# One padded tile, one result tile and one transposing transfer for queries and keys in a clustered-attention kernel

## The chip, the cores and the metric

The kernel runs on one core of a Trainium2 chip. The metric is the time of one launch in microseconds of device time, as a median of runs. One execution was taken with the hardware profiler; its rows are quoted below. TensorE multiplies, VectorE, ScalarE and GpSimd do the elementwise work, and the sync engine (SP) issues almost all transfers, in order, on one queue.

## The reference

Sixteen heads (2 batches of 8), 768 positions, 64 columns. Each query and each key belongs to the centroid (of 16) with which it has the largest product. A query sees the keys of its own cluster only. Two dense layers with softplus, and two with a leaky rectifier, follow.

```python
q_assign = argmax(einsum('bhsd,hcd->bhsc', q_n, c_n)); k_assign = argmax(einsum('bhsd,hcd->bhsc', k_n, c_n))
mask = q_assign[:, :, :, None] == k_assign[:, :, None, :]
scores = where(mask, matmul(q, k.T) / sqrt(D), -1e9)
attn = exp(scores - max(scores)); attn = attn / (sum(attn) + 1e-9)
x = (attn @ v).transpose(0, 2, 1, 3).reshape(1536, 512)
x = softplus(x @ w_in) @ w_out            # 512 -> 2048 -> 512
out = leaky(x @ w_in2) @ w_out2           # 512 -> 2048 -> 512
```

The weights come in 64-bit floats, which the kernel decodes itself.

## The kernel before

Every fp32 operand is carried as two fp16 parts, a high one and the rest. A head goes through these steps (h is the head, 0 to 15; C = 6 blocks of 128 positions):

- `load(h)` brings queries and keys into `qk`.
- `split(h)`: ScalarE casts queries into the first 64 columns of a padded tile `nq` and keys into those of `nk` (line 294), GpSimd takes the rests (line 295), ScalarE copies the high parts (line 296); all four go into `n1`. One transposing transfer of twelve 128 x 128 blocks turns `n1` into `t1` (line 298; the profile calls it t<-n).
- `assign_mm(h)` and `assign_el(h)`: products with the centroids (line 307), the largest of 16 on VectorE, and the cluster as 16 columns of 0 or BIG, which ScalarE writes beside the high parts in `nq` and `nk` (lines 329 and 330). Two transposing transfers of six blocks each, `nq` to `tq` (line 333) and `nk` to `tk` (line 334). A query and a key of one cluster then get BIG more in their product than others.
- `emit_s1(h, c)`: the masked products of the high parts (line 346), of which VectorE takes row maxima (line 353). `emit_m(h)` writes these maxima into further rows of `tq` (lines 360 to 375), so that the next product subtracts them.
- `emit_s2(h, j)`: scores by two products (lines 393 and 394), their exponentials on ScalarE (line 400), the rests on GpSimd (line 402).
- `emit_pv`: products with the values (lines 416 to 434); `emit_empty(h)`: a last product that reads `tq` (line 452) and corrects rows whose cluster has no key.
- `emit_norm(h)`: division, and the result of two heads side by side in `xnh` and `xnl`. `emit_out` transposes each (line 456) into `xt_h[b]` and `xt_l[b]`, what the first dense layer reads (`layer_in`, line 698). `layer_mid` (line 711) is the second layer.

The order of each engine's instructions is fixed when the kernel is built: a planner simulates the program and takes, of what it believes ready, what has the lowest number in `at_pri`. Head h has numbers around h: its split at h - 2.5, its row maxima at h - 4, its scores at h. From head 8 on, steps of the dense layers of the first batch are mixed in (`moe_steps`). `w_step` loads and decodes one 512 KB piece of the first two layers' weights; two pieces can be in flight.

On the sync queue some transfers are ordered behind another one: `behind_tk(h)` puts what is issued under it behind the transfer kept in `tki[h]`, which is line 334's. Under it stand, in turn h, the loads of the values of head h + 2, the finished output pair, and the weight pieces of the turn; all pieces that are left in turn 11 stand behind `tki[13]`.

Tiles rotate. `BUFS` names for each tag how many tiles there are that last and how many only in heads 0 to 7 (`atile`): the turn goes round both kinds until head 7, then round the lasting ones. `tq` has (3, 2), `tk` (3, 1). The padded tiles are fixed ones (`padded`): `nq` (2, 2), `nk` (2, 1). A tile is taken over when its last reader is done; for `tq` that is line 452 of the head before in the turn, for `nq` and `nk` the transposing transfer.

Of the kernel before, what the change touches and what calls it, by code (L numbers as in the profile page):

```python
# [9 lines left out]
F16 = mybir.dt.float16  # L10
BF16 = mybir.dt.bfloat16
I32 = mybir.dt.int32
AF = mybir.ActivationFunctionType
ALU = mybir.AluOpType
# [4 lines left out]
BIG = 32768.0  # L19
# [3 lines left out]


BUFS = {
# [4 lines left out]
}  # L30
NQ_BUFS, NK_BUFS, V_BUFS = (2, 2), (2, 1), 3
PSUM_BUFS = {"as": 1, "s1": 2, "s2": 2}


# [1 line left out]
HI = ("AA", "AA", "AA", "AA", "AA", "AA")  # L36
DUP = ("AA", "AA", "AA", "AA", "AA", "AA")
# [14 lines left out]
def by_group(table, h):  # L52
    return table[min(h // 2, 4 + (h >= 12))]
# [3 lines left out]
def attn_moe_kernel(  # L57
# [12 lines left out]
    nc = tc.nc  # L70
    V, S, G, PE = nc.vector, nc.scalar, nc.gpsimd, nc.tensor
    B, H, SEQ, D = q.shape
    NCL = cen.shape[1]
    DM, DFF = w_in1.shape
    C = SEQ // 128
    KDM, KFF = DM // 128, DFF // 128
    NH = B * H
    TB = 384
    scale = 1.0 / float(D) ** 0.5
# [4 lines left out]
    const = ctx.enter_context(tc.tile_pool(name="const", bufs=1))  # L84
# [5 lines left out]
    ep = actx.enter_context(tc.tile_pool(name="ep", bufs=1, reuse_waits="tile"))  # L90
    acon = bctx.enter_context(tc.tile_pool(name="acon", bufs=1, side="right", reuse_waits="tile"))
# [6 lines left out]
    def atile(shape, dt, tag, h):  # L98
        late, early = BUFS[tag]
        n = turn[tag] = turn.get(tag, -1) + 1  # L100
        if h < H and early and n % (late + early) >= late:
            return ep.tile(shape, dt, tag=tag, name=tag, bufs=early)
        return at.tile(shape, dt, tag=tag, name=tag, bufs=late)
# [2 lines left out]
    w_inl = const.tile([128, KDM, DFF], F16, name="w_inl")  # L106
    w_outh = const.tile([128, KFF, DM], F16, name="w_outh")
    w_outl = const.tile([128, KFF, DM], F16, name="w_outl")
    xt_h = [const.tile([128, KDM, SEQ], F16, name=f"xth{b}") for b in range(B)]
    xt_l = [const.tile([128, KDM, SEQ], F16, name=f"xtl{b}") for b in range(B)]  # L110
    def padded(bufs, name):
        n, late = sum(bufs), bufs[0]
        tiles = [(acon if i < late else ep).tile([128, C, 128], F16, name=f"{name}_{i}") for i in range(n)]
        return tiles, [tiles[h % n if h < H else (h - H) % late] for h in range(NH)]

    nqs, nq_of = padded(NQ_BUFS, "nq")
    nks, nk_of = padded(NK_BUFS, "nk")
    v2s = [acon.tile([128, C, 2 * D + 1], F16, name=f"v2_{i}") for i in range(V_BUFS)]
    v32s = [acon.tile([128, C, D + 1], F32, name=f"v32_{i}") for i in range(V_BUFS)]
    mms = [acon.tile([128, C, 3], F32, name=f"mm{i}") for i in range(2)]  # L120
# [14 lines left out]
    mark, tki = {}, {}  # L135
    ld_t, tp1, tp2, tpq, p_t, xn_t, as_t, x_t, v_t, svs = ({} for _ in range(10))
# [141 lines left out]
    def load_v(h):  # L278
        b, hh = divmod(h, H)
        vv = v32s[h % V_BUFS][:, :, 0:D]  # L280
        nc.sync.dma_start(out=vv, in_=v[b, hh].rearrange("(p c) d -> p c d", c=C))
        v_t[h] = vv
# [5 lines left out]

    def split(h):
        qk = ld_t.pop(h)  # L290
        nq, nk = nq_of[h], nk_of[h]
        n1 = atile([128, C, 4, D], F16, "n1", h)
        for t_, n_ in enumerate((nq, nk)):
            (S.copy if by_group(HI, h)[t_] == "A" else V.tensor_copy)(out=n_[:, :, 0:D], in_=qk[:, t_])
            G.tensor_tensor(out=n1[:, :, 1 + t_, :], in0=qk[:, t_], in1=n_[:, :, 0:D], op=ALU.subtract)
            (S.copy if by_group(DUP, h)[t_] == "A" else V.tensor_copy)(out=n1[:, :, 3 * t_, :], in_=n_[:, :, 0:D])
        t = atile([128, 2 * C, 128], F16, "t1", h)
        nc.sync.dma_start_transpose(out=t, in_=n1.rearrange("p c s d -> p (c s d)"))
        tp1[h] = t
# [13 lines left out]
                )  # L313

    def assign_el(h):
        nq, nk = nq_of[h], nk_of[h]
        aps = as_t.pop(h)
        a, e = (aps[:, n:n + 2 * C * NCL].rearrange("p (i j) -> p i j", j=NCL) for n in (0, 2 * C * NCL))
        mx = atile([128, 2 * C, 1], F32, "mx", h)
        V.reduce_max(out=mx, in_=a, axis=AX)  # L320
        V.tensor_tensor(out=e, in0=a, in1=mx.to_broadcast([128, 2 * C, NCL]), op=ALU.is_equal)
        V.tensor_tensor(out=e, in0=e, in1=tab, op=ALU.mult)
        m2 = atile([128, 2 * C, 1], F32, "m2", h)
        V.reduce_max(out=m2, in_=e, axis=AX)
        oh = atile([128, C, 2, NCL], F16, "oh", h)
        V.tensor_tensor(
            out=oh.rearrange("p c t j -> p (c t) j"), in0=e, in1=m2.to_broadcast([128, 2 * C, NCL]), op=ALU.is_equal
        )
        S.activation(out=nq[:, :, D:D + NCL], in_=oh[:, :, 0, :], func=AF.Copy, scale=BIG, bias=-BIG)
        S.activation(out=nk[:, :, D:D + NCL], in_=oh[:, :, 1, :], func=AF.Copy, scale=BIG)  # L330
        tk = atile([128, C, 128], F16, "tk", h)
        t = atile([128, C, 128], F16, "tq", h)
        nc.sync.dma_start_transpose(out=t, in_=nq.rearrange("p c d -> p (c d)"))
        tki[h] = nc.sync.dma_start_transpose(out=tk, in_=nk.rearrange("p c d -> p (c d)"))
        tp2[h] = t, tk

    KS1 = D + NCL
    MR = 96
# [112 lines left out]
        for c in range(C):  # L451
            PE.matmul(out=xps[:, c * XW:(c + 1) * XW], lhsT=t[MR:KS2, c, :], rhs=r[MR:KS2, :], start=False, stop=(c == C - 1))

    def emit_out(b, hh, xh, xl):
        for src, dst in ((xh, xt_h[b]), (xl, xt_l[b])):
            nc.sync.dma_start_transpose(
                out=dst[:, hh // 2, :].rearrange("p (c r) -> p c r", c=C), in_=src.rearrange("p c d -> p (c d)")
            )

    outs_t = {}  # L460

    def emit_norm(h):
        b, hh = divmod(h, H)
        if hh % 2 == 0:
            xn_t[h // 2] = [atile([128, C, 128], F16, f"xn{n}", h) for n in "hl"]
        xh, xl = xn_t[h // 2]
        xps = x_t.pop(h)
        xv = xps[:, 0:C * XW].rearrange("p (c d) -> p c d", d=XW)
        dp = xps[:, C * XW:C * XW + C].unsqueeze(2)
        dd = atile([128, C, 1], F32, "dd", h)  # L470
        V.tensor_scalar(out=dp, in0=xv[:, :, D:XW], scalar1=1e-9, scalar2=1.0 / XS, op0=ALU.add, op1=ALU.mult)
        V.reciprocal(out=dd, in_=dp)
        y = atile([128, C, D], F32, "y", h)
        V.tensor_tensor(out=y, in0=xv[:, :, 0:D], in1=dd.to_broadcast([128, C, D]), op=ALU.mult)  # L474
        cs = slice((hh % 2) * D, (hh % 2) * D + D)
        S.copy(out=xh[:, :, cs], in_=y)
        G.tensor_tensor(out=xl[:, :, cs], in0=y, in1=xh[:, :, cs], op=ALU.subtract)
        for d_ in (tp1, tp2, tpq):
            d_.pop(h)
        if hh % 2 == 1:  # L480
            xn_t.pop(h // 2)
            if hh < H - 1:
                outs_t[h + 2] = b, hh, xh, xl
            else:
                with at_pri(h + 1 - LEAD_NORM):
                    emit_out(b, hh, xh, xl)

# [3 lines left out]
    late, w2 = {}, {}  # L491
# [237 lines left out]
    @contextmanager  # L729
    def at_pri(x):  # L730
        old = tc.cur_priority
        tc.cur_priority = pri(x)
        yield
        tc.cur_priority = old
# [8 lines left out]
    with at_pri(-9):  # L743
# [6 lines left out]
            out=ss[:, 1:2], in0=ss[:, 0:1], scalar1=ss[:, 2:3], scalar2=ss[:, 1:2], op0=ALU.mult, op1=ALU.add  # L750
# [8 lines left out]
    load(1)  # L759
    load_v(0)  # L760
    load_v(1)
    for n_ in nqs + nks:
        with tc.issue_after(centred.ins):
            V.memset(n_[:, :, D:128], 0.0)
    for n_ in nks:
        with tc.issue_after(centred.ins):
            V.memset(n_[:, :, MR:MR + C], -1.0)
    for v3 in v32s:
        G.memset(v3[:, :, D:D + 1], 1.0)
    for v2 in v2s:  # L770
# [3 lines left out]
        out=ident, in_=ones, pattern=[[1, 128]], compare_op=ALU.is_equal, fill=0.0, base=0, channel_multiplier=-1  # L774
# [4 lines left out]
    for j in range(NCL):  # L779
# [4 lines left out]
        out=sel, in_=sel, pattern=[[0, 1]], compare_op=ALU.is_ge, fill=0.0, base=-MR - 2 * C, channel_multiplier=1  # L784
# [112 lines left out]
    def chain(h):  # L897
        if h < NH:
            with at_pri(h - LEAD_SPLIT):
                split(h)  # L900
            with at_pri(h - LEAD_ASSIGN):
                assign_mm(h)
                assign_el(h)
            with at_pri(h - LEAD_MAX):
                for c in range(C):
                    emit_s1(h, c)
            if h + 2 < NH:
                with at_pri(h - LEAD_LOAD):
                    load(h + 2)
# [12 lines left out]
    for h in range(NH):  # L922
# [28 lines left out]
        with at_pri(h + 1 - LEAD_NORM):  # L951
            emit_norm(h)
# [49 lines left out]
```

## Time and profile before

| | before |
|---|---|
| median of 3 runs | 740.99 us (739.66 to 744.81) |
| the profiled execution's own time | 746.45 us |
| its span, first to last instruction | 744.7 us |
| busy: TensorE / VectorE / ScalarE / GpSimd | 682.4 / 517.1 / 413.9 / 402.0 us |
| granted TensorE clock, mean over the span | 0.984 of full |
| transposing transfers of lines 298, 333, 334, 456 | 16, 16, 16 and 16 |

The span is what the rows are counted in; the profiled execution is somewhat longer than the median, so a sum is made against 746.45 and then carried over to 740.99. Attention lasts to about 330 us, the rest is dense layers.

### The profile page before, as it was taken

To read this page: it belongs to the slowest core of one execution; us is meant where nothing else is said; L and a number is where in the kernel's file an instruction comes from. 1 tells how busy PE (TensorE), PEld (TensorE's weight loads), DVE (VectorE), ACT (ScalarE), POOL (GpSimd) and SP (SyncE) were. 2 spreads that over 40 slices of the span, in tenths; PEclk is the share of its full clock that TensorE was granted. 3 is DMA by queue.
4 is the path that set the end of the run, shared out by engine and by line. 5 is a ranking of instruction groups with operands and counts; after the bars stand their busy time and mean duration, and the time that the engine had idled before them with its cause. 6 is when DMAs were issued, how large, how long until landed. Compare 5 with 4: busy or idle time off the path is not lost. (4 is left out here: it accounts for less than half of the span.)

```text
span 744.7 us, 19022 instructions
## 1 busy us (share of the span) xinstructions
PE 682.4 (92%) x7584; PEld 508.9 (68%) x7584; DVE 517.1 (69%) x1169; ACT 413.9 (56%) x1089; POOL 402.0 (54%) x494
## 2 busy tenths in 40 slices
PE   1798999979878999989999899999999999999997
PEld 1365767655546666656666566657999999999996
DVE  4796788878877983138878867967475766665545
ACT  5574676758767863266235524625555555565553
POOL 5385787759767874222314332334655555556553
PEclk9998999999989999999999999999999999999999
DMA  8986855695473654012322255696200000000000
GB/s 201 207 176 149 143 126 110 147 180 120 131 161 100 158 133 80 1 22 85 114 85 84 87 192 168 209 318 214 89 2 30 2 30 2 30 2 30 2 30 29
DMA packets 105289, 77.88 MB, mean 105 GB/s; under 512 B 79088, under 2 KB 93424, under 8 KB 105200
## 3 DMA queue, kind: packets, MB, share of 16 engines
q1 hardware_dynamic: 105056, 76.40, 40.4%
q8 instruction: 59, 0.97, 0.6%
q14 instruction: 30, 0.25, 0.1%
q10 hardware_dynamic: 144, 0.26, 0.1%
HBM read 50.36 MB, written 10.49 MB: 82 GB/s over the span
## 5 line engine op out<-in xcount | busy, mean ns | idle before, releaser
L402 POOL TENSOR_TENSOR pl<-p 128x768 f16<-128x768 f32 x88 | 128.3, 1468 | 49.3 <-ACT p L400 31.4
L353 DVE TENSOR_REDUCE mm<-s 128x1 f32<-128x384 f32 x190 | 100.6, 548 | 25.7 <-PE s L346 25.0
L563 PEld LDWEIGHTS <-w_in2h 128*128 128x128 f16 x1344 | 98.2, 98 | 6.3 <-issue 1.7
L571 DVE TENSOR_TENSOR gl<-r,gh 128x384 f16<-128x384 f32 (+1 forms) x96 | 63.7, 664 | 49.6 <-ACT gh L609 48.9
L400 ACT ACTIVATE p<-s 128x384 f32<-128x384 f32 x160 | 74.8, 494 | 34.1 <-PE s L394 30.1
L698 PE MATMUL m<-xth,w_inh 128*128 128x384 f16 x256 | 84.8, 332 | 3.9 <-DVE y L474 1.5
L711 PE MATMUL m<-g_l,w_outh 128*128 128x384 f16 x256 | 83.4, 326 | 3.1 <-DVE g_l L512 3.1
L698 PE MATMUL m<-xtl,w_inh 128*128 128x384 f16 x256 | 85.1, 333 | 0.0
L711 PE MATMUL m<-g_h,w_outh 128*128 128x384 f16 x256 | 83.5, 326 | 0.2 <-ACT rl L522 0.2
L711 PE MATMUL m<-g_h,w_outl 128*128 128x384 f16 x256 | 83.3, 326 | 0.0
L571 POOL TENSOR_TENSOR r<-r,r 128x128 f32<-128x128 f32 x95 | 48.3, 526 | 55.7 <-ACT r L601 55.4
L698 PEld LDWEIGHTS <-w_inh 128*128 128x128 f16 x512 | 50.1, 99 | 36.1 <-issue 4.2
L609 ACT CAST gh<-r 128x384 f16<-128x384 f32 (+1 forms) x96 | 54.2, 565 | 35.8 <-POOL r L571 32.5
L711 PEld LDWEIGHTS <-w_outh 128*128 128x128 f16 x512 | 49.7, 98 | 32.7 <-ACT w_outh L163 0.4
L346 PE MATMUL s<-tk,tq 128*128 128x384 f16 x190 | 61.4, 346 | 10.2 <-DVE mm L353 6.3
L563 PEld LDWEIGHTS <-gh 128*128 128x128 f16 x672 | 60.5, 98 | 6.4 <-issue 1.1
L201 POOL TENSOR_TENSOR wd<-wd 128x256 f32<-128x256 f32 x32 | 29.3, 924 | 55.7 <-DVE sg L195 41.1
L393 PE MATMUL s<-t 128*128 128x384 f16 x160 | 53.7, 335 | 5.4 <-ACT p L400 5.0
L394 PE MATMUL s<-tq,tk 128*128 128x384 f16 x160 | 53.7, 336 | 0.2 <-ACT tq L375 0.2
L563 PE MATMUL i<-sh,w_in2h 128*128 128x128 f16 x384 | 53.5, 219 | 0.3 <-ACT r L601 0.3
L563 PE MATMUL i<-sl,w_in2h 128*128 128x128 f16 x384 | 53.5, 219 | 0.0
L563 PE MATMUL i<-sh,w_in2l 128*128 128x128 f16 x384 | 53.4, 219 | 0.0
(154 smaller groups left out, 1950.1 us busy)
## 6 DMA issues: line engine op xcount, KB each, us to landing
st<-in_moe_w_in_dram SPq DMA_DIRECT2D x32, 512.0 KB, 4.2
st<-in_moe_w_out_dram SPq DMA_DIRECT2D x32, 512.0 KB, 3.8
kept<-sg SPq DMA_DIRECT2D x16, 256.0 KB, 2.9
qk<-in_q_dram SPq DMA_DIRECT2D x16, 192.0 KB, 3.3
qk<-in_k_dram SPq DMA_DIRECT2D x16, 192.0 KB, 3.0
v<-in_v_dram SPq DMA_DIRECT2D x16, 192.0 KB, 4.0
kept<-sg SPq DMA_DIRECT2D x24, 128.0 KB, 2.7
out_dram<-ob SPq DMA_DIRECT2D x11, 256.0 KB, 2.0
```

What stands on the lines that cost most here:

```text
L201: G.tensor_tensor(out=out, in0=in0, in1=in1, op=ALU.subtract)
L346: PE.matmul(out=o, lhsT=t[:, c, :], rhs=tk[:, 3 * j:3 * j + 3, :], start=True, stop=True,)
L353: V.reduce_max(out=mms[h % 2][:, c, j:j + 1], in_=bank[:, 0:3 * 128], axis=AX)
L393: PE.matmul(out=o, lhsT=t1[:, kt, 1, :], rhs=t1[:, 3 * j:3 * j + 3, 0, :], start=True, stop=False)
L394: PE.matmul(out=o, lhsT=t2[:, kt, :], rhs=tqh[:, 3 * j:3 * j + 3, :], start=False, stop=True)
L400: S.activation(out=p[:, j, :], in_=sp, func=AF.Exp, scale=scale)
L402: G.tensor_tensor(out=pl, in0=p, in1=pb, op=ALU.subtract)
L563: one = PE.matmul(out=bank, lhsT=w_, rhs=x_, start=(first and i == 0), stop=(i == len(ops) - 1), skip_group_check=True)
L571: eng.tensor_tensor(out=out, in0=in0, in1=in1, op=op)
L609: S.copy(out=gh[:, lo:hi], in_=r[:, lo:hi])
L698: PE.matmul(out=hp, lhsT=w_, rhs=x_, start=(i == 0), stop=(i == len(ops) - 1))
L711: PE.matmul(out=yp, lhsT=w_[:, kk, ms], rhs=g_[:, kk, :], start=(n == 0), stop=(n == 3 * KFF - 1))
```

## The change

Queries and keys of a head share one padded tile of two halves, and one result tile of two halves. One transposing transfer of twelve blocks takes the place of the two of six. It waits for the columns of both (lines 329 and 330), and for the result tile's last reader of either half. The ring of padded tiles has 2 + 2 (as `nq` had; `nk` had 2 + 1), the ring of result tiles 3 + 1 (as `tk` had; `tq` had 3 + 2). `tki[h]` is now the merged transfer. In the same way the two parts of an output pair share one tile `xn` and one transfer of twelve blocks into one tile `xt[b]`, of which `xt_h[b]` and `xt_l[b]` are views. The choice of engine in `split` by table goes; the tables named ScalarE everywhere.

```diff
-    "qk": (2, 1), "n1": (1, 2), "t1": (4, 2), "tq": (3, 2), "tk": (3, 1),
+    "qk": (2, 1), "n1": (1, 2), "t1": (4, 2), "tq": (3, 1),
...
-    "dd": (2, 0), "y": (2, 0), "xnh": (2, 0), "xnl": (2, 0),
+    "dd": (2, 0), "y": (2, 0), "xn": (2, 0),
 }
-NQ_BUFS, NK_BUFS, V_BUFS = (2, 2), (2, 1), 3
+N_BUFS, V_BUFS = (2, 2), 3
...
-    xt_h = [const.tile([128, KDM, SEQ], F16, name=f"xth{b}") for b in range(B)]
-    xt_l = [const.tile([128, KDM, SEQ], F16, name=f"xtl{b}") for b in range(B)]
+    xt = [const.tile([128, KDM, 2, SEQ], F16, name=f"xt{b}") for b in range(B)]
+    xt_h, xt_l = ([t[:, :, n] for t in xt] for n in range(2))
...
-    nqs, nq_of = padded(NQ_BUFS, "nq")
-    nks, nk_of = padded(NK_BUFS, "nk")
+    ns, n_of = padded(N_BUFS, "nq")
...
-        for t_, n_ in enumerate((nq, nk)):
-            (S.copy if by_group(HI, h)[t_] == "A" else V.tensor_copy)(out=n_[:, :, 0:D], in_=qk[:, t_])
-            G.tensor_tensor(out=n1[:, :, 1 + t_, :], in0=qk[:, t_], in1=n_[:, :, 0:D], op=ALU.subtract)
-            (S.copy if by_group(DUP, h)[t_] == "A" else V.tensor_copy)(out=n1[:, :, 3 * t_, :], in_=n_[:, :, 0:D])
+        for t_ in range(2):
+            S.copy(out=n_[:, t_, :, 0:D], in_=qk[:, t_])
+            G.tensor_tensor(out=n1[:, :, 1 + t_, :], in0=qk[:, t_], in1=n_[:, t_, :, 0:D], op=ALU.subtract)
+            S.copy(out=n1[:, :, 3 * t_, :], in_=n_[:, t_, :, 0:D])
...
-        tk = atile([128, C, 128], F16, "tk", h)
-        t = atile([128, C, 128], F16, "tq", h)
-        nc.sync.dma_start_transpose(out=t, in_=nq.rearrange("p c d -> p (c d)"))
-        tki[h] = nc.sync.dma_start_transpose(out=tk, in_=nk.rearrange("p c d -> p (c d)"))
-        tp2[h] = t, tk
+        t = atile([128, 2, C, 128], F16, "tq", h)
+        tki[h] = nc.sync.dma_start_transpose(
+            out=t.rearrange("p t c r -> p (t c) r"), in_=n_.rearrange("p t c d -> p (t c d)")
+        )
+        tp2[h] = t[:, 0], t[:, 1]
...
-    def emit_out(b, hh, xh, xl):
-        for src, dst in ((xh, xt_h[b]), (xl, xt_l[b])):
-            nc.sync.dma_start_transpose(
-                out=dst[:, hh // 2, :].rearrange("p (c r) -> p c r", c=C), in_=src.rearrange("p c d -> p (c d)")
-            )
+    def emit_out(b, hh, xn):
+        nc.sync.dma_start_transpose(
+            out=xt[b][:, hh // 2].rearrange("p n (c r) -> p (n c) r", c=C), in_=xn.rearrange("p n c d -> p (n c d)")
+        )
```

## Rows read from the trace of the kernel before

**Rows 1.** The page's first line: the span.
```profile
span 744.7 us, 19022 instructions
```
**Rows 2.** Busy time by stage: stretch, length, busy per engine, clock, DMA share, GB/s.
```profile
20.00:40.00 20.00, 16.27 (x137) 9.28 (x136) 15.54 (x37) 11.10 (x29) 8.54 (x9) 1.00 1.05 218
40.00:140.00 100.00, 90.38 (x1317) 67.14 (x1315) 80.96 (x195) 65.58 (x164) 74.23 (x62) 0.97 0.64 133
140.00:280.00 140.00, 122.11 (x1470) 81.28 (x1467) 116.27 (x241) 101.58 (x243) 105.20 (x93) 0.95 0.64 144
...
330.00:744.00 414.00, 404.07 (x4124) 318.14 (x4121) 285.57 (x632) 205.00 (x590) 185.47 (x291) 1.00 0.26 83
```
**Rows 3.** Waits of the whole span: engine, line, releaser; total, times, longest.
```profile
PE as L307 <- DMA t<-n: 17.4, 6, 11.7
...
ACT nk L294 <- DMA tk<-nk: 15.7, 11, 3.6
...
ACT nq L294 <- DMA tq<-nq: 8.9, 5, 3.6
...
PE s L346 <- DMA tq<-nq: 1.7, 1, 1.7
```
**Rows 4.** Timeline of the sync queue: start, us of issue, line, transfer.
```profile
87.94 1.25 SPq L333 DMA_TRANSPOSE tq<-nq  x1
...
110.40 1.22 SPq L334 DMA_TRANSPOSE tk<-nk  x1
...
119.91 1.25 SPq L333 DMA_TRANSPOSE tq<-nq  x1
...
139.09 1.21 SPq L334 DMA_TRANSPOSE tk<-nk  x1
...
146.99 1.22 SPq L333 DMA_TRANSPOSE tq<-nq  x1
...
205.54 1.22 SPq L334 DMA_TRANSPOSE tk<-nk  x1
...
213.28 3.97 SPq L154 DMA_DIRECT2D st<-in_moe_w_out_dram  x2
...
220.35 1.22 SPq L333 DMA_TRANSPOSE tq<-nq  x1
```
**Rows 5.** Timeline of TensorE: last products of heads 3, 5 and 10.
```profile
95.86 0.35 PE L452 MATMUL x<-svr,tq 32*128 32x65 f16 x6
...
119.53 0.35 PE L452 MATMUL x<-svr,tq 32*128 32x65 f16 x6
...
219.97 0.35 PE L452 MATMUL x<-svr,tq 32*128 32x65 f16 x6
```
**Rows 6.** DMA issues of the whole span: count, median us from issue to landing.
```profile
t<-n SPq DMA_TRANSPOSE x16, 4.4
tq<-nq SPq DMA_TRANSPOSE x16, 2.8
tk<-nk SPq DMA_TRANSPOSE x16, 3.0
```
**Rows 7.** Lines 298 and 333 on the queue: least, median, longest ns.
```profile
L298 SPq DMA_TRANSPOSE t<-n x16: 1431/1634/3637, 7.9 to 230.6; - x16
...
L333 SPq DMA_TRANSPOSE tq<-nq x16: 1216/1248/2588, 15.6 to 261.0; - x16
```
**Rows 8.** Timeline of TensorE: head 7's first product for row maxima.
```profile
114.47 0.32 PE L346 MATMUL s<-tk,tq 128*128 128x384 f16 x1
```
**Rows 9.** Timeline around 150 us: in brackets idle time and what ended it.
```profile
153.64 0.51 ACT L294 CAST nq<-qk 128x384 f16<-128x384 f32 x1 [3.61 <-DMA tq<-nq]
...
155.55 0.32 PE L393 MATMUL s<-t 128*128 128x384 f16 x1 [2.44 <-ACT p L400]
```
**Rows 10.** Timeline: second layer's first product, last weight piece's conversion.
```profile
261.14 0.32 PE L711 MATMUL m<-g_h,w_outh 128*128 128x384 f16 x1 [0.20 <-ACT rl L522]
...
283.72 0.60 ACT L163 ACTIVATE w_outh<-wcp 128x512 f16<-128x512 f32 x1
```

More of the change, by code (lines that the diff above doesn't have):

```diff
@@ L108, in attn_moe_kernel @@
     w_outl = const.tile([128, KFF, DM], F16, name="w_outl")
-    xt_h = [const.tile([128, KDM, SEQ], F16, name=f"xth{b}") for b in range(B)]
-    xt_l = [const.tile([128, KDM, SEQ], F16, name=f"xtl{b}") for b in range(B)]
+    xt = [const.tile([128, KDM, 2, SEQ], F16, name=f"xt{b}") for b in range(B)]
+    xt_h, xt_l = ([t[:, :, n] for t in xt] for n in range(2))
     def padded(bufs, name):
         n, late = sum(bufs), bufs[0]
-        tiles = [(acon if i < late else ep).tile([128, C, 128], F16, name=f"{name}_{i}") for i in range(n)]
+        tiles = [(acon if i < late else ep).tile([128, 2, C, 128], F16, name=f"{name}_{i}") for i in range(n)]
         return tiles, [tiles[h % n if h < H else (h - H) % late] for h in range(NH)]
-    nqs, nq_of = padded(NQ_BUFS, "nq")
-    nks, nk_of = padded(NK_BUFS, "nk")
+    ns, n_of = padded(N_BUFS, "nq")
     v2s = [acon.tile([128, C, 2 * D + 1], F16, name=f"v2_{i}") for i in range(V_BUFS)]
@@ L290, in split @@
         qk = ld_t.pop(h)
-        nq, nk = nq_of[h], nk_of[h]
+        n_ = n_of[h]
         n1 = atile([128, C, 4, D], F16, "n1", h)
-        for t_, n_ in enumerate((nq, nk)):
-            (S.copy if by_group(HI, h)[t_] == "A" else V.tensor_copy)(out=n_[:, :, 0:D], in_=qk[:, t_])
-            G.tensor_tensor(out=n1[:, :, 1 + t_, :], in0=qk[:, t_], in1=n_[:, :, 0:D], op=ALU.subtract)
-            (S.copy if by_group(DUP, h)[t_] == "A" else V.tensor_copy)(out=n1[:, :, 3 * t_, :], in_=n_[:, :, 0:D])
+        for t_ in range(2):
+            S.copy(out=n_[:, t_, :, 0:D], in_=qk[:, t_])
+            G.tensor_tensor(out=n1[:, :, 1 + t_, :], in0=qk[:, t_], in1=n_[:, t_, :, 0:D], op=ALU.subtract)
+            S.copy(out=n1[:, :, 3 * t_, :], in_=n_[:, t_, :, 0:D])
         t = atile([128, 2 * C, 128], F16, "t1", h)
@@ L315, in assign_el @@
     def assign_el(h):
-        nq, nk = nq_of[h], nk_of[h]
+        n_ = n_of[h]
         aps = as_t.pop(h)
@@ L328, in assign_el @@
         )
-        S.activation(out=nq[:, :, D:D + NCL], in_=oh[:, :, 0, :], func=AF.Copy, scale=BIG, bias=-BIG)
-        S.activation(out=nk[:, :, D:D + NCL], in_=oh[:, :, 1, :], func=AF.Copy, scale=BIG)
-        tk = atile([128, C, 128], F16, "tk", h)
-        t = atile([128, C, 128], F16, "tq", h)
-        nc.sync.dma_start_transpose(out=t, in_=nq.rearrange("p c d -> p (c d)"))
-        tki[h] = nc.sync.dma_start_transpose(out=tk, in_=nk.rearrange("p c d -> p (c d)"))
-        tp2[h] = t, tk
+        S.activation(out=n_[:, 0, :, D:D + NCL], in_=oh[:, :, 0, :], func=AF.Copy, scale=BIG, bias=-BIG)
+        S.activation(out=n_[:, 1, :, D:D + NCL], in_=oh[:, :, 1, :], func=AF.Copy, scale=BIG)
+        t = atile([128, 2, C, 128], F16, "tq", h)
[3 more added lines that the diff above has]
+        tp2[h] = t[:, 0], t[:, 1]
     KS1 = D + NCL
@@ L464, in emit_norm @@
         if hh % 2 == 0:
-            xn_t[h // 2] = [atile([128, C, 128], F16, f"xn{n}", h) for n in "hl"]
-        xh, xl = xn_t[h // 2]
+            xn_t[h // 2] = atile([128, 2, C, 128], F16, "xn", h)
+        xn = xn_t[h // 2]
+        xh, xl = xn[:, 0], xn[:, 1]
         xps = x_t.pop(h)
@@ L482, in emit_norm @@
             if hh < H - 1:
-                outs_t[h + 2] = b, hh, xh, xl
+                outs_t[h + 2] = b, hh, xn
             else:
                 with at_pri(h + 1 - LEAD_NORM):
-                    emit_out(b, hh, xh, xl)
+                    emit_out(b, hh, xn)
     pmx = [pm]
@@ L761, in attn_moe_kernel @@
     load_v(1)
-    for n_ in nqs + nks:
+    for n_ in ns:
         with tc.issue_after(centred.ins):
-            V.memset(n_[:, :, D:128], 0.0)
-    for n_ in nks:
+            V.memset(n_[:, :, :, D:128], 0.0)
+    for n_ in ns:
         with tc.issue_after(centred.ins):
-            V.memset(n_[:, :, MR:MR + C], -1.0)
+            V.memset(n_[:, 1, :, MR:MR + C], -1.0)
     for v3 in v32s:
```

## The prediction

> **What bounds the kernel now.** I read the span and the busy times by stage first [rows 1, 2]. From 330 us on TensorE is busy 404.07 of 414 us, so nothing this edit does can be felt there unless the work before it ends later. The edit lives in attention, up to about 330 us, and there TensorE leaves 20 − 16.27 = 3.73 us open in the stage 20 to 40 us, 100 − 90.38 = 9.62 us in 40 to 140 and 140 − 122.11 = 17.89 us in 140 to 280. The granted clock averages 0.97 and 0.95 of full in the last two, between its levels of 2.4 and 1.2 GHz; that is another 3 and 7 us of full-speed work lost. A gain has to come out of these gaps, about 31 us in all (4% of the span), and a loss shows as more of them: TensorE takes its instructions in a fixed order, so each wait that the planner did not foresee is idle time.
>
> Then the waits [rows 3]: transposing transfers hold ScalarE for 15.7 us at the key copies and 8.9 us at the query copies (line 294, which must not overwrite a padded tile before its transfer has read it). TensorE itself waits little for the transfers in question: 1.7 us once for a query transfer at the row-maximum products, and 17.4 us in 6 waits for the first transposition of a head, 11.7 of them at the start.
>
> Last, each head's transfers in order of issue on the sync queue; the k-th issue of a line is head k. In heads 0 to 7 the query transfer and the key transfer go out back to back. From head 8 on they part: head 8's key transfer goes at 110.40 and its query transfer at 119.91, head 13's at 205.54 and 220.35 [rows 4]. The reason stands in the row of line 452 just before: 119.53 and 219.97 [rows 5]. A query tile is read up to the last product of its head, the correction for empty rows, and head 8 takes over the tile of head 5, head 13 that of head 10.
>
> **The edit, part by part.**
>
> *One transfer for two.* A transposition of six blocks lands 2.8 us (queries) or 3.0 us (keys) after issue, one of twelve blocks (the first transposition of a head, the nearest row) 4.4 us [rows 6]. On the queue six blocks take 1.248 us and twelve 1.634 [rows 7]. A back-to-back pair is complete 1.25 + 3.0 = 4.25 us after the first issue, the merged one 4.4 us: no change for heads 0 to 7, and the product that reads it needs both parts. The queue is relieved of 2 × 1.25 − 1.63 = 0.87 us for each of 24 pairs (16 heads, 8 outputs), 21 us in all. That counts only where TensorE waits for something on this queue: after the start 17.4 − 11.7 = 5.7 us for first transpositions and 1.7 us for a query transfer, 7.4 us [rows 3]. An earlier issue can hardly end more than half of these. Value taken: −0.5 us on the path (0 to −3.7). The output pairs are read long after their transfers but for the last one of the first batch; by the same blocks they count nothing.
>
> The completion comes with the last byte, and that speaks against joining where one half was already there. Heads 11 to 15 have their keys early; there the merged transfer lands 4.4 − 2.8 = 1.6 us after what used to end the wait. The Trainium skill, page "DMA: Bandwidth & Descriptors", section "Anatomy of one DMA — SWDGE (gpsimd) path", says the semaphore cannot fire until the last byte is confirmed in place; the rows agree, 2.8 against 4.4 us.
>
> What do 1.6 us cost? Nothing if the planner foresaw them. The nearest row for a twelve-block transfer with TensorE at its end is the first transposition: (17.4 − 11.7) / 5 = 1.1 us each wait [rows 3]. Five heads, 0 to 5 × 1.6 = 8 us; I take 2.
>
> *Places in the rings.* Both tables get new counts. The merged result tile has 3 + 1 tiles in heads 0 to 7 where queries had 3 + 2 and keys 3 + 1. So heads 5 to 7 now wait for the head four before, not five. The worst is head 7: its transfer goes from 87.94 [rows 4] to after head 3's last product, 95.86 [rows 5], 8 us later. Its first reader runs at 114.47 [rows 8], 15 us after the landing then; the row-maximum products of the heads before it cover that, so it costs nothing. If that cover were gone it would be up to 8 us.
>
> In heads 8 to 10 the turn of the ring helps: they take the tile of the head four before instead of three. Head 8 goes when its data are there (110.40, as its keys do now) instead of 119.91. Head 10 could go by about 139 (its keys' time, 139.09) instead of 146.99 [rows 4]. That touches the costliest gap of the stage: ScalarE stood 3.61 us until 153.64, because the next user of the padded query tile waited for that late transfer, and the exponentials behind it on ScalarE kept TensorE 2.44 us [rows 9]. With the transfer 8 us earlier this wait has no cause. Value: −3.5 us, the 2.44 and about 1 us of the half-speed clock of this stage; between 0 (the planner makes another one) and −6 (the whole 2.44 and half of the 7 us).
>
> *Four padded tiles for keys, not three.* The copies of the key part in heads 3 to 9 now wait for the head four before. That takes away most of the 15.7 us [rows 3], but ScalarE is busy 65.58 of 100 us there [rows 2] and few of those waits reached TensorE. Value −1 us, 0 to −3.
>
> In heads 10 to 15 the ring has two tiles as before. There the key copies become as late as the query copies are now, so their one copy and one subtraction join the queries' burst; the first transposition needs both anyway.
>
> *What stands behind the merged transfer.* Line 334's instruction is also a marker: loads of the values, loads of the weight pieces and the output transposition are ordered behind it on the sync queue (`behind_tk`). In heads 11 to 15 the marker moves from the key transfer's time to the query transfer's. Behind head 13's stand the last twelve weight pieces: the first load is at 213.28 and would be after 220.35 + 1.63 = 222.0, 8.7 us later [rows 4]. The last piece of these is converted at 283.72, and the second layer, which reads the pieces one by one, has its first product at 261.14 [rows 10]: it is paced by them. VectorE, which decodes them, is busy 116.27 of 140 us [rows 2], so it has 24 us with which to catch up, and TensorE has the attention of heads 13 to 15 to do meanwhile. Value +2 us, between 0 and 8.7.
>
> **Sum.** −0.5 + 2 − 3.5 − 1 + 2 = −1.0 us. The extremes add up to −3.7 − 6 − 3 = −12.7 and +8 + 8.7 = +16.7. The profiled execution took 746.45 us, 5.5 us more than the median of the runs, 740.99; the edit makes 745.45 of it, which is 740.0 on the median.
>
> **The rivals.**
>
> *Slower: the marker.* The one mechanism: the held transfer of heads 11 to 13 keeps weight loads behind it, the second layer's first block ends 8.7 us later, and what TensorE finds instead is attention at its own pace, which does not fill it (122.11 of 140). Time 741 + 8.7 = 750. It decides when VectorE does not make up the delay before 280 us. For it: the pieces come just in time now [rows 10]. Against: VectorE's spare time, and that the order is planned anew.
>
> *Faster: the gaps close.* Heads 8 to 10 run ahead, the stall at 150 us goes with its half-speed stretch (−6), the key copies' waits give 3 and the start 1: 741 − 10 = 731. For it: the stall's chain is plain [rows 9]. Against: in a fixed order one stall is soon replaced by another.
>
> *Joining pays by itself.* Two of six blocks and one of twelve give 2 × 2.8 − 4.4 = 1.2 us of fixed time for each transfer saved. If all 24 lay on the path, 741 − 29 = 712 us. The rows speak against it: TensorE's wait for a query transfer is 1.7 us [rows 3]. The Trainium skill, same page, section "Rules for kernel authors", advises to join many small transfers because below 64 KB one pays mostly overhead; the fixed 1.2 us agrees, but whether it is paid in time is a matter of the path.
>
> That the merged transfer takes no less than the two is already in the sum, which has no gain from landing earlier.
>
> **How the numbers follow.** The unchanged time has 0.47. The marker rival has 0.24. The closing gaps have 0.27 and the joining rule 0.02. A measurement of this kernel tells about 1% (7.4 us) from no change; so faster 0.29, same 0.47, slower 0.24. The forecast is 740.0. The likeliest case alone spans 734 to 748. The range leaves out the joining rule, and the outer end of either rival: the faster rival's 731 with the rest of the bounds (741 − 12.7 = 728), the slower one's 750 with part of the late landings (4 of the 8 us), 754.
>
> **What would show it.** One transposing transfer for each head, 1.4 to 1.7 us on the queue and about 4.4 us to landing, and one for each output pair. Head 8's near 110 us and head 10's before 140; the 3.61 us of ScalarE and the 2.44 us of TensorE gone, and the key copies' 15.7 us shrunk. Heads 11 to 15 right after line 452 of the head three before, with TensorE waiting up to 1.6 us at line 346's product. The weight loads behind head 13 after 220 us, the last conversion no later than 290. I am wrong if the busy share in 330 to 744 changes, if the clock dips elsewhere by more than 7 us, or if the new order puts a wait on TensorE that none of these transfers ends.

## The result, and the profile after

The changed kernel takes 733.39 us (median of 6 runs, 731.3 to 736.26) and the kernel before 741.94 us (6 runs, 739.66 to 744.81): a ratio of 0.9879 with a 95% interval of 0.9851 to 0.9907, so 1.2% faster, 8.5 us. The forecast was 740.0. The rival in which the gaps close (731) came nearest. Medians and ratios below leave out one slow execution (762.43 us, of the kernel before with the scores' halves turned).

The profiled execution of the changed kernel took 732.15 us. Its page gives the span, and busy time and instructions of TensorE:

```profile
span 730.4 us, 18968 instructions
...
PE 677.0 (93%) x7584; PEld 506.7 (69%) x7584; DVE 517.3 (71%) x1167; ACT 410.9 (56%) x1087; POOL 402.5 (55%) x494
```

Against [rows 1] the span is 14.3 us shorter. That is more than the medians' 8.5, because the profiled execution before lay 4.5 us above its median and that of the changed kernel 1.2 us below. The parts below add up to 14.3, and only their proportions carry over. TensorE ran the same 7584 instructions in 677.0 us of busy time instead of 682.4. The other 14.3 - 5.4 = 8.9 us are idle time that went. The 5.4 us go with a higher clock (mean over the span 0.996 instead of 0.984), but they are not clock alone: with two writes swapped (below) the kernel before is busy 675.1 us, less than the changed one, at a mean clock of 0.990.

Where it went is read in busy time by stage (columns as in [rows 2]). First the changed kernel:

```profile
20.00:40.00 20.00, 16.21 (x107) 8.30 (x108) 15.08 (x37) 11.12 (x29) 7.86 (x9) 1.00 1.08 215
40.00:140.00 100.00, 92.54 (x1401) 70.46 (x1400) 84.23 (x202) 67.51 (x170) 77.43 (x63) 1.00 0.71 145
140.00:280.00 140.00, 124.53 (x1550) 83.78 (x1547) 116.96 (x241) 104.53 (x250) 108.92 (x95) 0.99 0.60 146
280.00:345.00 65.00, 64.44 (x512) 40.29 (x510) 30.16 (x59) 26.86 (x58) 15.09 (x11) 1.00 0.13 35
...
140.00:160.00 20.00, 17.56 (x260) 12.07 (x256) 19.35 (x41) 14.16 (x33) 13.61 (x12) 1.00 0.69 147
...
240.00:260.00 20.00, 17.75 (x161) 11.37 (x160) 14.72 (x29) 12.14 (x29) 14.20 (x13) 0.91 0.60 129
...
330.00:730.00 400.00, 391.90 (x4048) 310.75 (x4046) 276.30 (x609) 198.53 (x573) 186.34 (x291) 1.00 0.26 84
```

Then stretches of the kernel before that [rows 2] do not hold, in the same columns:

```profile
60.00:80.00 20.00, 18.50 (x228) 12.87 (x228) 14.62 (x37) 11.05 (x28) 9.18 (x8) 0.83 0.78 148
...
140.00:160.00 20.00, 14.18 (x200) 9.76 (x198) 17.30 (x36) 11.21 (x27) 12.42 (x11) 0.96 0.88 181
...
180.00:200.00 20.00, 17.04 (x212) 11.11 (x211) 16.18 (x35) 15.39 (x39) 15.71 (x16) 0.91 0.60 129
200.00:220.00 20.00, 17.03 (x177) 10.65 (x177) 15.54 (x32) 14.54 (x35) 14.54 (x14) 0.91 0.77 165
220.00:240.00 20.00, 17.06 (x223) 11.77 (x222) 14.94 (x33) 13.75 (x36) 14.54 (x13) 0.91 0.41 104
...
280.00:345.00 65.00, 61.94 (x564) 39.69 (x563) 22.19 (x51) 27.80 (x59) 18.27 (x15) 1.00 0.18 38
```

TensorE is busy 2.16 us more in 40 to 140, 2.42 us more in 140 to 280 and 2.50 us more in 280 to 345, and nothing more at the start. (Equal times do not hold equal work; the last stretch holds more of the dense layers in the changed kernel.) The granted clock rose from 0.97 to 1.00 and from 0.95 to 0.99 in the first two: the 0.83 at 60 to 80 us and the 0.91 of three slices after 180 us are gone, and one 0.91 at 240 us is left. So attention is over sooner. Its last product on TensorE stood at 325.28 us before and stands here, as the last row, in the changed kernel's timeline:

```profile
92.35 0.35 PE L451 MATMUL x<-svr,tq 32*128 32x65 f16 x6
...
138.53 0.93 ACT L293 CAST nq<-qk 128x384 f16<-128x384 f32 x2 [0.17 <-DMA tq<-nq]
...
204.93 0.35 PE L451 MATMUL x<-svr,tq 32*128 32x65 f16 x6
...
254.40 0.33 PE L710 MATMUL m<-g_h,w_outh 128*128 128x384 f16 x1
...
275.48 0.60 ACT L162 ACTIVATE w_outh<-wcp 128x512 f16<-128x512 f32 x1
...
313.35 0.35 PE L451 MATMUL x<-svr,tq 32*128 32x65 f16 x6
```

The 325.28 is a row of the kernel before of the same form:

```profile
325.28 0.35 PE L452 MATMUL x<-svr,tq 32*128 32x65 f16 x6
```

That is 11.9 of the 14.3 us; behind it 744.7 - 325.28 = 419.4 us and 730.4 - 313.35 = 417.1 us remain. From 330 us on the busy share is 391.90 / 400 = 98.0% against 97.6% before.

The waits of the whole span, to be read beside [rows 3]:

```profile
ACT nq L293 <- DMA tq<-nq: 17.0, 10, 3.3
PE as L306 <- DMA t<-n: 14.5, 5, 11.7
...
PE s L345 <- DMA tq<-nq: 4.5, 3, 2.3
```

Two waits of TensorE in the kernel before that [rows 3] do not hold:

```profile
PE s L346 <- DMA tk<-nk: 1.4, 1, 1.4
...
PE m L698 <- DMA xth<-xnh: 1.3, 1, 1.3
```

The issues from issue to landing, and the merged transfer's line on the queue, beside [rows 6, 7]:

```profile
t<-n SPq DMA_TRANSPOSE x16, 4.3
tq<-nq SPq DMA_TRANSPOSE x16, 3.9
xt<-xn SPq DMA_TRANSPOSE x8, 4.9
...
L331 SPq DMA_TRANSPOSE tq<-nq x16: 1274/1454/2492, 16.3 to 244.7; - x16
```

And the sync queue's timeline: the merged transfers of heads 7, 8, 9, 10 and 13, and the weight load behind the last of them, beside [rows 4]:

```profile
93.38 1.43 SPq L331 DMA_TRANSPOSE tq<-nq  x1
107.67 1.45 SPq L331 DMA_TRANSPOSE tq<-nq  x1
121.39 1.47 SPq L331 DMA_TRANSPOSE tq<-nq  x1
134.81 1.60 SPq L331 DMA_TRANSPOSE tq<-nq  x1
...
205.31 1.44 SPq L331 DMA_TRANSPOSE tq<-nq  x1
206.84 0.82 SPq L153 DMA_DIRECT2D st<-in_moe_w_out_dram  x1
```

### The profile page after: what moved, and what is told of

It is laid out like the page before. It is cut to its first block, busy times and chain, and to the rows that moved or that the text cites. A ratio compares the mean times of both kernels' runs of the same rounds, so it can differ in the third digit from the quotient of the medians.

```text
span 730.4 us, 18968 instructions
## 1 busy us (share of the span) xinstructions
PE 677.0 (93%) x7584; PEld 506.7 (69%) x7584; DVE 517.3 (71%) x1167; ACT 410.9 (56%) x1087; POOL 402.5 (55%) x494
## 5 line engine op out<-in xcount | busy, mean ns | idle before, releaser
L697 PE MATMUL m<-xt,w_inh 128*128 128x384 f16 x512 | 93.8, 326 | 4.2 <-ACT rl L521 3.4
L345 PE MATMUL s<-tq 128*128 128x384 f16 x190 | 62.0, 345 | 9.3 <-DMA tq<-nq 4.5
L562 PE MATMUL i<-xt,w_in2h 128*128 128x128 f16 x576 | 57.2, 219 | 0.1
L393 PE MATMUL s<-tq 128*128 128x384 f16 x160 | 53.2, 333 | 1.6 <-ACT tq L374 1.6
```

What stands on the lines that cost most here:

```text
L345: PE.matmul(out=o, lhsT=t[:, c, :], rhs=tk[:, 3 * j:3 * j + 3, :], start=True, stop=True,)
L393: PE.matmul(out=o, lhsT=t2[:, kt, :], rhs=tqh[:, 3 * j:3 * j + 3, :], start=False, stop=True)
L562: one = PE.matmul(out=bank, lhsT=w_, rhs=x_, start=(first and i == 0), stop=(i == len(ops) - 1), skip_group_check=True)
L697: PE.matmul(out=hp, lhsT=w_, rhs=x_, start=(i == 0), stop=(i == len(ops) - 1))
```

## The experiments

Three theories. *Counts* ("rings" in the expectations): the new numbers of tiles (a fourth padded key tile, and the turn that lets heads 8 to 10 go early) close the gaps, and the joining itself pays nothing. *Joining*: fewer transfers on the queue pay. *Redraw* ("plan"): the planner orders everything anew after any edit, and part of the 1.2% is the luck of the new order. When the first four runs did not add up, the third was put to the test by itself. Each of the twelve kernels was timed in five rounds against the kernel before on the same chip; ratios are to that kernel, with 95% intervals. First the edit was taken apart.

**Outputs alone.** The kernel before, with the output half of the change.

```diff
-    "dd": (2, 0), "y": (2, 0), "xnh": (2, 0), "xnl": (2, 0),
+    "dd": (2, 0), "y": (2, 0), "xn": (2, 0),
...
+        nc.sync.dma_start_transpose(
+            out=xt[b][:, hh // 2].rearrange("p n (c r) -> p (n c) r", c=C), in_=xn.rearrange("p n c d -> p (n c d)")
+        )
```

> Only the output pairs share a tile and a transfer; queries and keys as before. Rings (the gain comes from which tile a head takes over: heads 8 to 10 four heads back): no change, 742 us within 3. Joining (each transfer saved pays): 8 of 24 transfers, a third of the 8.5 us gained, about 739 us. Plan (any edit makes the planner draw another order, and the result scatters): anywhere from 735 to 749 us, with no tie to what was edited.

Measured: 739.41 us, 0.9959 (0.994 to 0.9979). Small, on the gaining side, and within all three forecasts.

**Queries and keys alone.** The changed kernel, with the outputs of before.

```diff
-    "dd": (2, 0), "y": (2, 0), "xn": (2, 0),
+    "dd": (2, 0), "y": (2, 0), "xnh": (2, 0), "xnl": (2, 0),
...
+        for src, dst in ((xh, xt_h[b]), (xl, xt_l[b])):
+            nc.sync.dma_start_transpose(
+                out=dst[:, hh // 2, :].rearrange("p (c r) -> p c r", c=C), in_=src.rearrange("p c d -> p (c d)")
+            )
```

> Only queries and keys share tiles and a transfer; output pairs as before. Rings: the whole gain, 733 to 735 us, and head 10's transfer before 140 us. Joining: two thirds of the gain, about 736 us. Plan: 730 to 749 us.

Measured: 742.61 us, 1.0 (0.9981 to 1.002): no gain at all, which neither *counts* nor *joining* had. The parts do not add, 0.9959 x 1.0 against 0.9879. Up to about 145 us this run keeps up with the changed kernel. Then its timeline has two short waits of TensorE and behind them a long one of ScalarE, and the clock of the next stretch falls:

```profile
152.73 0.32 PE L697 MATMUL m<-xth,w_inh 128*128 128x384 f16 x1 [1.27 <-DMA xth<-xnh]
...
159.67 0.27 PE L306 MATMUL as<-ct,t 128*128 128x16 f16 x4 [2.87 <-DMA t<-n]
...
163.94 0.49 ACT L520 ACTIVATE mr<-m 128x384 f32<-128x384 f32 x1 [5.47 <-PE m L697]
```

Busy time by stage of the same kernel, the ten us with that wait:

```profile
160.00:170.00 10.00, 10.00 (x104) 6.21 (x103) 6.84 (x16) 5.61 (x15) 3.29 (x3) 0.85 0.09 17
```

The first product of a dense step stood in front of attention's products and waited 1.27 us for an output transfer. The loss that follows is longer than that wait; I read it as the work of the order behind it, which is not shown by a run of its own.

**Counts alone.** The kernel before, all transfers separate, with the changed kernel's numbers of tiles.

```diff
-    "qk": (2, 1), "n1": (1, 2), "t1": (4, 2), "tq": (3, 2), "tk": (3, 1),
+    "qk": (2, 1), "n1": (1, 2), "t1": (4, 2), "tq": (3, 1), "tk": (3, 1),
...
-NQ_BUFS, NK_BUFS, V_BUFS = (2, 2), (2, 1), 3
+NQ_BUFS, NK_BUFS, V_BUFS = (2, 2), (2, 2), 3
```

> Separate tiles and separate transfers as before, only the counts of the changed kernel: results of queries 3 + 1, padded keys 2 + 2. Rings: most of the gain, 733 to 737 us, with head 8's query transfer at about 110 us and no 3.6 us wait of ScalarE at 150 us. Joining: no gain, 742 us. Plan: 730 to 749 us.

Measured: 734.52 us, 0.9894 (0.9866 to 0.9922). This is the changed kernel's gain without one transfer joined, as *counts* had it.

**One tile, two transfers.** The changed kernel; each half of the merged tile is moved by itself.

```diff
-        tki[h] = nc.sync.dma_start_transpose(
-            out=t.rearrange("p t c r -> p (t c) r"), in_=n_.rearrange("p t c d -> p (t c d)")
-        )
+        for t_ in range(2):
+            tki[h] = nc.sync.dma_start_transpose(out=t[:, t_], in_=n_[:, t_].rearrange("p c d -> p (c d)"))
```

> The changed kernel, but the joined query-key tile is moved by two transfers of six blocks, back to back. Rings: as the changed kernel, 732 to 736 us. Joining: 8.5 x 16/24 = 5.7 us of the gain lost, about 739 us. Plan: 730 to 749 us.

Measured: 738.66 us, 0.9943 (0.9919 to 0.9968), 0.6% behind the changed kernel. By itself this would speak for joining; the run above, with separate transfers, speaks against it. The four mixtures of parts lay between 1.0 and 0.9894 in no order that any part explains, so the next ones split the counts and asked how much a mere change of order makes.

**The query ring alone.** The kernel before, with one result tile fewer for queries.

```diff
-    "qk": (2, 1), "n1": (1, 2), "t1": (4, 2), "tq": (3, 2), "tk": (3, 1),
+    "qk": (2, 1), "n1": (1, 2), "t1": (4, 2), "tq": (3, 1), "tk": (3, 1),
```

> The kernel before with one count changed: results of queries 3 + 1 in place of 3 + 2, so that heads 8 to 10 take the tile of the head four before (and heads 5 to 7 lose one). Rings, queries' part: most of what the counts alone gave (734.5 of 742.7), so 734 to 737 us, head 8's query transfer near 108 us. Rings, keys' part: if the fourth padded key tile made the gain, no change, 742 us. Plan: 730 to 749 us.

Measured: 748.77 us, 1.0089 (1.0059 to 1.0119): slower, which neither side of *counts* had, though the query transfers of heads 8 and 10 went early, at 107.28 and 136.25 us. From this kernel to "counts alone" only the fourth padded key tile is added, and ScalarE's waits for padded tiles shrink. The waits of this one:

```profile
ACT nk L294 <- DMA tk<-nk: 19.9, 12, 2.7
...
ACT nq L294 <- DMA tq<-nq: 4.7, 6, 3.1
```

and of "counts alone":

```profile
ACT nq L294 <- DMA tq<-nq: 11.3, 7, 2.6
...
ACT nk L294 <- DMA tk<-nk: 2.8, 6, 0.8
```

24.6 us became 14.1 us, and the ratio fell from 1.0089 to 0.9894, some 14 us. Most of the loss of the query ring alone sits at the end of attention. Its busy time by stage:

```profile
280.00:345.00 65.00, 59.11 (x489) 36.99 (x488) 17.87 (x41) 30.91 (x58) 14.57 (x11) 0.92 0.09 18
...
300.00:320.00 20.00, 16.55 (x159) 10.62 (x157) 2.79 (x5) 15.21 (x23) 6.78 (x5) 1.00 0.00 1
320.00:330.00 10.00, 7.55 (x60) 4.55 (x60) 0.93 (x3) 2.14 (x6) 3.81 (x3) 0.57 0.21 41
```

In 300 to 320 ScalarE is busy 15.21 us and TensorE stands 3.45 us; then the clock falls to 0.57. From about 315 us the last head's attention runs with no dense products left to fill in, and TensorE waits for the exponentials and their rests, as in these rows of its timeline:

```profile
317.84 0.36 PE L434 MATMUL x<-v,pl 128*128 128x65 f16 x6 [0.81 <-POOL pl L402]
...
320.21 0.32 PE L393 MATMUL s<-t 128*128 128x384 f16 x1 [2.01 <-ACT p L400]
```

**The turn undone.** The changed kernel, with the places of the ring shifted so that heads 8 to 10 take over the tile of the head three before, as in the kernel before.

```diff
-        if h < H and early and n % (late + early) >= late:
+        if h < H and early and (n + 3 * (tag == "tq")) % (late + early) >= late:
```

> The changed kernel, with the one extra result tile given to heads 0 and 4 in place of 3 and 7, so that heads 8 to 10 take the tile of the head three before, as in the kernel before. Rings, queries' part: the gain goes, 738 to 743 us, with head 8's transfer after head 5's last product (about 115 us) and head 10's after head 7's. Keys' part or joining: stays 731 to 736 us. Plan: 730 to 749 us.

Measured: 738.64 us, 0.9963 (0.994 to 0.9986). The merged transfers of heads 8 to 10 are late again:

```profile
116.66 1.97 SPq L331 DMA_TRANSPOSE tq<-nq  x1
134.06 1.43 SPq L331 DMA_TRANSPOSE tq<-nq  x1
147.15 2.66 SPq L331 DMA_TRANSPOSE tq<-nq  x1
```

and TensorE is busy 122.11 us in 140 to 280, where the changed kernel has 124.53 and the kernel before 122.11 [rows 2]. By this run the turn gives 0.9963 - 0.9879 = 0.84% of 742, 6.2 us.

**Counts and outputs.** "Counts alone" with the joined outputs added.

> The counts of the changed kernel with separate query and key transfers, and joined output pairs. If the parts add (0.9894 and 0.9959): 0.985, 732 us, faster than the changed kernel. If the plan decides: no sum, anywhere from 730 to 745 us.

Measured: 734.71 us, 0.9907 (0.9873 to 0.9941). The outputs add nothing here. Joining queries and keys on top of this is the changed kernel, 0.9879, level within the intervals; without the joined outputs the same step went from 0.9894 to 1.0. A part costs 1.1% in one neighbourhood and nothing in the other.

**Two neutral writes.** The kernel before with lines 329 and 330 in the other order. Nothing else differs, and neither waits for the other.

```diff
-        S.activation(out=nq[:, :, D:D + NCL], in_=oh[:, :, 0, :], func=AF.Copy, scale=BIG, bias=-BIG)
         S.activation(out=nk[:, :, D:D + NCL], in_=oh[:, :, 1, :], func=AF.Copy, scale=BIG)
+        S.activation(out=nq[:, :, D:D + NCL], in_=oh[:, :, 0, :], func=AF.Copy, scale=BIG, bias=-BIG)
```

> The kernel before with two neighbouring ScalarE instructions of 0.28 us swapped (the keys' 16 columns written before the queries'). The work is the same, the planner draws another order. Rings or joining: 742 us within 2, since neither counts nor transfers change. Plan: a scatter of the size of the gain itself, up to 9 us either way.

Measured: 736.95 us, 0.9931 (0.9903 to 0.996). An edit with no content is worth 0.7%, more than half of what is to be explained. TensorE's order differs in most places from about 58 us to the end of attention. Its busy time, in all and at the end of attention:

```profile
PE 675.1 (92%) x7584; PEld 505.6 (69%) x7584; DVE 516.5 (70%) x1169; ACT 412.8 (56%) x1087; POOL 402.6 (55%) x494
...
280.00:345.00 65.00, 65.00 (x500) 40.44 (x499) 28.80 (x57) 27.16 (x60) 14.89 (x11) 1.00 0.14 39
```

This kernel has three padded key tiles, like the query ring alone, and no late end. So the same kind of edit was made in pairs, to the kernel before and to the changed one.

**Halves of the maxima, before and after.** In `emit_m` the second half is written first.

```diff
-        for j in range(2):
+        for j in (1, 0):
             bank = ring("s2", h)
```

> The kernel before, the two halves of the row maxima written in the other order (same work, another order drawn by the planner). Edit itself pays: about 742 us (within 3), so that the same redraw of the changed kernel is 9 us faster. Plan: between 733 and 749 us, and the pair's difference is anywhere between -9 and +9.

> The changed kernel with the same redraw. Edit itself pays: about 733 us (within 3). Plan, the first draw having been lucky: 736 to 745 us.

Measured: 739.06 us, 0.9959 (0.9934 to 0.9984), and 736.71 us, 0.9923 (0.9895 to 0.9951). The changed kernel's place in this pair is what *redraw* had (736 to 745).

**Halves of the scores, before and after.** The same in `emit_s2`.

```diff
-        for j in range(2):
+        for j in (1, 0):
             sp = ring("s2", h)[:, 0:384]
```

> The kernel before, the two halves of a row of scores made in the other order: a second redraw. Edit itself pays: 9 us behind the next kernel. Plan: between 733 and 749 us.

> The changed kernel with the second redraw. Edit itself pays: 9 us ahead of the one before it in this list. Plan: 733 to 745 us, ahead or behind.

Measured: 750.95 us, 1.0115 (1.0079 to 1.0151), which lies outside every forecast, and 735.26 us, 0.9907 (0.9872 to 0.9942). The former has the same late end as the query ring alone. Its busy time by stage:

```profile
280.00:345.00 65.00, 58.86 (x496) 37.55 (x495) 16.46 (x38) 30.33 (x57) 14.41 (x11) 0.95 0.08 19
```

All orders together; the last column is the start of TensorE's last correction product (line 450, 451 or 452), read from each timeline:

| order | before, ratio | last product | changed, ratio | last product |
|---|---|---|---|---|
| as written | 1.0 | 325.28 | 0.9879 | 313.35 |
| maxima's halves turned | 0.9959 | 317.43 | 0.9923 | 319.29 |
| scores' halves turned | 1.0115 | 326.95 | 0.9907 | 313.77 |
| writes swapped | 0.9931 | 314.66 | | |

The mean is (1.0 + 0.9959 + 1.0115 + 0.9931) / 4 = 1.0001 for the kernel before and (0.9879 + 0.9923 + 0.9907) / 3 = 0.9903 for the changed one. The changed kernel is ahead in each pair: by 1.2%, by 1 - 0.9923 / 0.9959 = 0.4% (the intervals overlap) and by 1 - 0.9907 / 1.0115 = 2.1%. By their ratios its three orders lie below all four of the kernel before, though 0.9923 and 0.9931 cannot be told apart; that a given three of seven lie lowest has a chance of 1 in 35 if the orders are drawn blindly. So the edit is worth about 1% as an estimate. Four and three orders leave an uncertainty of nearly the same size, and a single pair tells less.

The other runs can be added to this. The seven kernels with both new counts (changed in three orders, queries and keys alone, counts alone, two transfers, counts and outputs) average 0.9922 and the six that keep three padded key tiles (before in four orders, outputs alone, query ring alone) 1.0009; the turn undone, with the new padded tile alone, is at 0.9963. Among the seven, the four that join queries and keys average 0.9927 and the three that move them in two transfers 0.9915: the joining shows no gain there.

Nor does the clock sort the kernels. Its mean over the profiled execution was highest, 0.997, for the kernel before with the maxima's halves turned (0.9959) and 0.995 for queries and keys alone (1.0), but 0.989 for counts alone (0.9894).

## Why the prediction was right or wrong, point by point

**The bound.** Right. Busy share after 330 us moved by 0.4 points, and 11.9 of the 14.3 us came before attention's last product, out of its gaps and its clock.

**One transfer for two.** Right in kind: it lands in 3.9 us (forecast 4.4) and keeps the queue 1.454 us (1.63). The prediction counted 1.7 us as TensorE's waits for the transfers that are joined; with those for a key transfer and for an output it was 1.7 + 1.4 + 1.3 = 4.4 us. The changed kernel has 4.5 us, all on the merged transfer, so nothing was lost where +2 was taken. The waits for first transpositions fell by 17.4 - 14.5 = 2.9 us where the queue's relief was given -0.5, inside its bound of -3.7; whether the queue or the new order did that is not shown. "Joining pays by itself" falls: counts alone give the gain with all transfers separate. The Trainium skill, page "DMA: Bandwidth & Descriptors", section "Rules for kernel authors", advises to join many small transfers and puts the overhead under 64 KB. Six blocks of 128 x 128 in fp16 are 192 KB, so the figure does not bear on these transfers. 0.9894 with separate ones and 0.9879 with joined ones have overlapping intervals; only the step from two transfers of one tile to one (0.9943 to 0.9879) points to a gain, and it is no larger than what a redrawn order gives.

**Heads 4 to 7 later.** Right: head 7's transfer at 93.38, just behind head 3's last product at 92.35 (head 4, which the prediction passes over, takes over head 0's tile now as well), and TensorE's busy time in 40 to 140 rose all the same.

**The turn of the ring.** Right: heads 8 and 10 at 107.67 and 134.81 (forecast near 110 and before 139), and TensorE's busy time in 140 to 160 up by 17.56 - 14.18 = 3.4 us, for -3.5 with the clock in it. The stall went too: the copy into the padded tile that head 10's transfer has read waited 0.17 us, until 138.53, instead of 3.61 us until 153.64 [rows 9]. The prediction put that stall down to a late issue alone; by [rows 4, 9] the transfer of 146.99 also took 153.64 - 146.99 = 6.65 us until it let the copy go, where the median is 2.8. The turn undone costs 6.2 us. That agrees, but the query ring alone had early transfers too and was slower, so early transfers alone do not make the gain, and 6.2 us is no more than a redrawn order can give.

**The fourth padded tile.** Perhaps the term that was sized too small. ScalarE's waits for padded tiles fell from 15.7 + 8.9 = 24.6 to 17.0 us, not by "most of the 15.7". But the reason given for -1 us, that few of those waits reached TensorE, counted only direct waits. Of the experiments, adding this tile made the largest step, 14 us, most of it at the end of attention, where TensorE waits for the exponentials. But the step is as wide as the whole scatter of redrawn orders (736.95 to 750.95), and with two writes swapped the kernel before has no late end although it lacks this tile. So neither the size of the term nor its sign is settled; the tile added alone to the kernel before was not run.

**The marker.** Here a step failed. The transfer of head 13 does go out right behind head 10's last product, as forecast, but at 205.31 instead of 220, since that product itself ran at 204.93 instead of 219.97 [rows 5]. The weight load behind it starts at 206.84, before the old 213.28, the second layer's first product at 254.40 and the last conversion at 275.48, both earlier than in [rows 10]. The term left head 10's last product at its old time, although the ring's own gain moves it (3.5 us were booked there; it moved by 15.0). The loads came earlier instead of 8.7 us later, so the +2 us had no cause left, and the slower rival hung on the same slip.

**The sum.** -1.0 us was forecast, -8.5 measured. The time lies in the range, but not in the likeliest case, whose 734 to 748 it just misses. Beside the marker, two entries were too small: the clock, entered with 1 us, where TensorE's busy time fell by 5.4 us in the profiled pair (not by clock alone), and the end of attention, which had no term, 2.5 us in 280 to 345. The sign of error named for the clock, a dip elsewhere by more than 7 us, did not come; one slice of 0.91 did. The faster rival's 731 is close partly by luck: its stall did close, but the start, to which it gave 1 us, gained nothing (16.21 us busy against 16.27), and the same kernel in another order takes 736.71. No bound had a term for the redrawn order, -0.7% to +1.15% without any reason in the edit, and the upper one also leaves out the 8 us named for head 7. About -1% on average over the orders is what the edit itself can claim, as an estimate.

**What stays open.** Which of the two counts carries the 1%, whether it is 1% or less, and the sign of each joined part: each is within what a redraw makes. No kernel of these beat the changed one; counts alone and counts with outputs are level with it.

## What to carry to other kernels

Where a planner writes the order, redraw it: swap two instructions that have nothing to do with each other, before and after, and credit an edit of 1% only when it holds over several such pairs. Count ring places by whose tile is taken over, not by their number alone, and when a step is freed early, move the steps that wait for it before pricing them. Price a gap as idle time, and ask whether a half-speed stretch may follow it.

## What the runs showed of the hardware

The same 7584 TensorE instructions were busy 682.4 us at a mean clock of 0.984, 677.0 us at 0.996 and 675.1 us at 0.990 (before, changed, two writes swapped): the clock alone does not set the busy time. Slices that averaged 0.83 and 0.91 ran in part at 1.2 instead of 2.4 GHz. In the query ring alone the clock averaged 0.57 in the 10 us that followed 20 us with 3.45 us of idle TensorE. Not every gap did that: in the kernel before, TensorE stood 2.74 us of these ten and the clock stayed up, in them and behind them:

```profile
320.00:330.00 10.00, 7.26 (x78) 4.81 (x76) 2.41 (x6) 6.62 (x12) 2.38 (x2) 1.00 0.11 21
```

A transposing transfer of twelve blocks landed after 3.9, 4.3 and 4.9 us (medians) depending on the tiles, not after one fixed time, and kept the queue from 1.27 to 2.49 us on one line.
